# Two attentions on one core: K and V of three batch-head pairs read with an outermost source dimension of 4, 4 and 2

## The chip, the cores and the metric

The kernel runs on one core of a Trainium2 chip. The metric is the device time of one execution in microseconds (us). A core has engines that run side by side: TensorE (PE, its weight loads shown as PEld), VectorE (DVE), ScalarE (ACT), GpSimd (POOL) and SyncE (SP). SP computes nothing; here it issues nearly all transfers. The transfers themselves run on 16 DMA engines, which are something else than the five above: "DMA engine" always means one of the 16 below.

## The reference, cut to what matters

Two attention blocks with a cached K and V, put side by side:

```python
def block(x, k_cache, v_cache, wq, wo):          # x: [16, 32, 1024], Dh = 128, 32 query heads
    q = (x @ wq) split into heads                # [16, 32, 32, 128]
    k, v = each cached head repeated for its query heads   # block A: 4 cached heads, block B: 32
    scores = q @ k^T * 128 ** -0.5               # over Sk = 1024 keys
    o = softmax(scores) @ v
    return (heads of o joined) @ wo              # [16, 32, 1024]
out = concatenate([block(A), block(B)], axis=-1)
```

Only the caches matter here. Block A reads 16 batches x 4 heads of K and V, each [1024 keys, 128] in bf16, 256 KB. Block B reads 16 x 32 of them, 256 MB in all. Softmax and the sum over keys do not depend on the order of the keys, as long as K and V of one batch and head are in the same order.

## The kernel before, in words

The work is cut into 128 steps. Step t has one "quad" of block A (a batch b, a cached head s, and four of the eight query heads that share it, so two quads in a row share one K and V) and, every second step, a pair of quads of block B with four K tiles and four V tiles of 512 KB.

**Loads.** A 512 KB tile of block B goes to 128 partitions with 4096 contiguous bytes each (`st_dmaKB` L904, `st_dmaVB` L949). K and V of block A go to 128 partitions with 2048 contiguous bytes each (`st_dmaKA` L885, `st_dmaVA` L892): partition p takes keys 8p to 8p+7. There are 64 loads of either kind. Weights are loaded in pieces of 256 and 512 KB (L708, L789, L799). Block B's K tiles have 8 buffers, its V tiles 6, block A's K and V two each, `KA_sb` and `VA_sb`, used in turn.

**What is done with them.** A K tile of block A is transposed by PE (L963) and evacuated to `KTA_sb`; scores are made by PE (L989), the row maximum by DVE (L1029), the exponential by ACT (L1042), P is transposed (L1054), and multiplied with V (L1074). A K tile of block B is transposed in place by DVE (L970), then scores (L1018), the same maximum and exponential, transposes (L1088) and the product with V (L1108). Projections stand at L729, L748 and L817.

**The order.** The program records every operation with what it reads and writes. `list_schedule` then places them one by one by modelled durations (a table for the engines; for transfers `dma_time`, bytes in packets over 16 DMA engines) and priorities, and this fixes the order of instructions on each engine. Waits follow from the order: a load waits on a semaphore of PE, ACT or DVE for its buffer to be free, and its first user waits for the load's own semaphore, which counts to 16. All these loads are issued by SP in one queue, in a fixed order, so that a load whose buffer is not free holds up those behind it. POOL issues seven of the output stores (L841).

Quads of block A are numbered by head first: quad t has s = t // 32 and b = 4 * ((t // 8) % 4) + (t % 8) // 2.

Of the kernel before, what the change touches and what calls it, by code (L numbers as in the profile page):

```python
# [546 lines left out]
def build(nc, pa, pb, out):  # L547
# [9 lines left out]
    NCH = Sk // P  # L557
# [22 lines left out]
    pr = Prog()  # L580
    stack = contextlib.ExitStack()
    with stack:
        def sb(name, shape, dt):
            return stack.enter_context(nc.sbuf_tensor(name, shape, dt))
# [20 lines left out]
        KA_sb = sb("KA_sb", [P, 2, NCH, Dh], BF)  # L605
        VA_sb = sb("VA_sb", [P, 2, NCH, Dh], BF)
# [257 lines left out]
        def mk_quadB(t):  # L864
# [13 lines left out]
            q.kid = ("B", t)  # L878
            return q

        def st_dmaKA(q):
            if not q.kv_new:
                return
            sl = q.kvslot
            pr.add("sp", lambda e: e.dma_start(KA_sb[:, sl, :, :], pa["k"][q.b, q.s].rearrange("(p c) d -> p c d", c=NCH)),  # L885
                   writes=[("KA", sl)], dma_key=f"ka{sl}", name="ka_dma", dur=Sk * Dh * 2, wtag={("KA", sl): q.kid})

        def st_dmaVA(q):
            if not q.kv_new:
                return  # L890
            sl = q.kvslot
            pr.add("sp", lambda e: e.dma_start(VA_sb[:, sl, :, :], pa["v"][q.b, q.s].rearrange("(p c) d -> p c d", c=NCH)),  # L892
                   writes=[("VA", sl)], dma_key=f"va{sl}", name="va_dma", dur=Sk * Dh * 2, wtag={("VA", sl): q.kid})

        def tile_src(key, x):
# [336 lines left out]
        def quadA_all(q):  # L1232
            t = q.t
            if q.kv_new:
                n1 = nextA(t, 1)
                if n1 is not None:
                    st_ktrA(n1)
                    n3 = nextA(t, 3)
                    if n3 is not None:
                        st_dmaKA(n3)  # L1240
                if n1 is not None and t >= 1:
                    st_dmaVA(n1)
            st_scoresA(q)
            st_max(q)
            st_exp(q)
            st_ptr(q)
            st_pev(q)
            st_pvA(q)
            st_recip(q)
            st_norm(q)  # L1250
            st_otr(q)
# [9 lines left out]
        for x in range(4):  # L1261
            st_dmaKB(x)
        st_dmaKA(quadsA[newA[0]])
        st_dmaVA(quadsA[newA[0]])
        for x in range(4):
            st_dmaVB(x)
        wo_loadB(0)
        lazy_pop(100)
        if len(newA) > 1:
            st_dmaKA(quadsA[newA[1]])  # L1270
            st_dmaVA(quadsA[newA[1]])
# [81 lines left out]
        if SCHED:  # L1353
            pr = pr.list_schedule()
# [10 lines left out]
def bass_concat_heads__gqa_block_cached__mha_block_cached__near_ridge_kernel(nc, A_x, A_k_cache, A_v_cache, A_wq, A_wo, B_x, B_k_cache, B_v_cache, B_wq, B_wo, out):  # L1365
    build(nc, dict(x=A_x, k=A_k_cache, v=A_v_cache, wq=A_wq, wo=A_wo),
          dict(x=B_x, k=B_k_cache, v=B_v_cache, wq=B_wq, wo=B_wo), out)
# [28 lines left out]
```

## Time and profile before

| what | value |
|---|---|
| time, median of 3 runs | 850.13 us (849.5 to 851.82) |
| time of the profiled execution | 851.77 us |
| its span, first to last instruction | 850.0 us (1.77 us lie around it) |
| busy share of the span: PE, DVE, ACT | 92%, 86%, 73% |
| granted TensorE clock | 0.998 |
| read from HBM, written | 337.64 MB, 2.10 MB |
| mean rate of all DMA | 402 GB/s |
| DMA queue of SP's loads, share of 16 DMA engines | 99.8% |

How to read it. Busy times are sums over an engine's instructions. The DMA share is the time that packets took, over 16 DMA engines and the span; a packet here is one contiguous run, 4096 or 2048 bytes for the loads above, and the next packet of an engine can start a few nanoseconds before the last one's end, which is why shares can pass 100%. "Landing" is the time at which a load's semaphore reaches its full count. Beside its views the trace holds a record of each DMA packet (queue, start, duration, size, but not which of the 16 engines) and the times of the sixteen increments of each load's semaphore, one from each DMA engine; they are called the packet records and the landing records below.

### The profile page before, as it was taken

The numbers are of one execution on the slowest core, as the hardware profiler recorded it, in microseconds if no ns is written. First come the engines' busy times: TensorE is split into PE (matmuls) and PEld (weight loads), VectorE is DVE, ScalarE is ACT, GpSimd is POOL, SyncE is SP. The second block draws the span as 40 slices with busy tenths as digits, with TensorE's granted clock in tenths as the row PEclk, the third lists the DMA queues.
The fourth block names the chain that finished last, engine by engine and source line by source line (L and its number), as shares of the span: only waits on it lengthen the run. The fifth ranks groups of instructions, "written<-read, shape, count | busy, mean of one in ns | idle before, by whom it ended". The sixth has DMA issues, their size and how long they took to land.

```text
span 850.0 us, 29762 instructions
## 1 busy us (share of the span) xinstructions
PE 781.1 (92%) x13056; PEld 519.9 (61%) x13056; DVE 734.1 (86%) x1025; ACT 622.9 (73%) x1356; POOL 6.1 (1%) x20
## 2 busy tenths in 40 slices
PE   6988989999899999999998998999999998989886
PEld 3456666666666566676565665566656666666654
DVE  1499898897898899998999789998899889998995
ACT  3378887876778767877777777686777758787864
POOL 1000000000000000000000000000000000000000
PEclk9999999999999999999999999999999999999999
DMA  9999999999999999999999999999999999999994
GB/s 331 415 404 411 412 411 416 415 400 354 409 414 411 415 412 411 415 397 413 408 416 414 413 406 403 415 403 414 413 404 411 410 411 407 416 415 414 416 417 187
DMA packets 112208, 341.68 MB, mean 402 GB/s; under 512 B 12048, under 2 KB 12304, under 8 KB 112080
## 3 DMA queue, kind: packets, MB, share of 16 engines
q1 hardware_dynamic: 111520, 337.95, 99.8%
q8 instruction: 103, 1.69, 0.7%
q0 software_dynamic: 560, 1.84, 0.5%
q14 instruction: 25, 0.20, 0.1%
HBM read 337.64 MB, written 2.10 MB: 400 GB/s over the span
## 4 chain that ended last, share of the span: by engine, by line
PE 53%; DVE 17%; DMA 15%; ACT 12%; issue 2%; SPq 1%; DVEq 0%; ACTq 0%
PE psum L1108 10%; PE psum L817 9%; DVE stat L1029 8%; ACT P_sb L1042 7%; DVE KB_sb L970 6%; DMA KB_sb<-in_B_k_cache_dram 6%; DMA VB_sb<-in_B_v_cache_dram 5%; PE psum L1018 5%; PE psum L1054 5%; PE psum L748 4%; PE psum L1088 4%; PE psum L989 4%; PE psum L729 4%; PE psum L1074 3%; PE psum L963 2%; DMA wq_sb<-in_B_k_cache_dram 2%
## 5 line engine op out<-in xcount | busy, mean ns | idle before, releaser
L1029 DVE TENSOR_REDUCE stat<-psum 128x1 f32<-128x1024 f32 x256 | 302.9, 1209 | 42.2 <-PE psum L989 25.3
L1042 ACT ACTIVATE P_sb<-psum,stat 128x1024 bf16<-128x1024 f32 x246 | 275.2, 1119 | 70.7 <-DVE stat L1029 67.8
L970 DVE STREAM_TRANSPOSE KB_sb<-KB_sb 128x1024 f32<-128x1024 f32 x240 | 289.7, 1226 | 17.3 <-DMA KB_sb<-in_B_k_cache_dram 16.8
L645 ACT COPY PT_sb<-psum 128x512 f32<-128x512 f32 x223 | 129.5, 598 | 39.7 <-PE psum L1088 22.2
L1108 PE MATMUL psum<-VB_sb,PT_sb 64*64 64x256 bf16 x3584 | 116.9, 271 | 11.9 <-ACT P_sb L1042 6.9
L1108 PEld LDWEIGHTS psum<-VB_sb,PT_sb 64*64 64x64 bf16 x3584 | 96.6, 107 | 33.0 <-issue 29.5
L1167 ACT ACTIVATE O_sb<-psum,stat 128x128 bf16<-128x128 f32 (+1 forms) x203 | 80.8, 418 | 35.4 <-PE psum L1074 16.1
L1054 PE MATMUL psum<-id,P_sb 128*128 128x128 f32 x512 | 88.5, 296 | 4.3 <-ACT P_sb L1042 3.0
L989 PE MATMUL psum<-KTA_sb,QT_sb 128*128 128x512 bf16 x256 | 82.0, 383 | 5.8 <-ACT P_sb L1042 2.6
L1054 PEld LDWEIGHTS psum<-id,P_sb 128*128 128x128 f32 x512 | 73.7, 208 | 19.5 <-ACT P_sb L1042 7.9
L1074 PE MATMUL psum<-VA_sb,PT_sb 128*128 128x128 bf16 x1024 | 77.8, 219 | 4.6 <-ACT P_sb L1042 1.9
L1088 PE MATMUL psum<-id,P_sb 128*128 128x128 f32 x472 | 78.1, 288 | 4.1 <-ACT P_sb L1042 1.1
L1074 PEld LDWEIGHTS psum<-VA_sb,PT_sb 128*128 128x128 bf16 x1024 | 62.5, 98 | 28.3 <-issue 12.3
L1018 PE MATMUL psum<-KB_sb,QR 32*32 32x512 bf16 x3840 | 72.7, 395 | 6.2 <-ACT P_sb L1042 5.4
L1088 PEld LDWEIGHTS psum<-id,P_sb 128*128 128x128 f32 x472 | 64.8, 193 | 20.1 <-ACT PT_sb L645 4.5
L748 PE MATMUL psum<-wq_sb,xT_sb 128*128 128x512 bf16 x256 | 73.0, 392 | 3.3 <-DMA wq_sb<-in_B_wq_dram 2.8
L817 PE MATMUL psum<-woB_sb,OTB_sb 128*128 128x512 bf16 x256 | 66.3, 380 | 3.6 <-ACT P_sb L1042 1.6
L817 PE MATMUL psum<-woA_sb,OTA_sb 128*128 128x512 bf16 x256 | 62.8, 380 | 2.2 <-ACT P_sb L1042 1.9
L1018 PEld LDWEIGHTS psum<-KB_sb,QR 32*32 32x32 bf16 x3840 | 43.6, 89 | 32.5 <-ACT P_sb L1042 9.8
L729 PE MATMUL psum<-xT_sb,wq_sb 128*128 128x512 bf16 x192 | 53.3, 379 | 0.5 <-ACT P_sb L1042 0.3
L1042 ACT ACTIVATION_READ_ACCUMULATOR P_sb<-psum,stat 128x1 f32 x246 | 49.6, 202 | 0.0
L829 DVE TENSOR_TENSOR acc<-acc,psum 128x512 f32<-128x512 f32 x64 | 41.2, 674 | 4.2 <-PE psum L817 4.2
(74 smaller groups left out, 718.3 us busy)
## 6 DMA issues: line engine op xcount, KB each, us to landing
KB_sb<-in_B_k_cache_dram SPq DMA_DIRECT2D x240, 512.0 KB, 9.6
VB_sb<-in_B_v_cache_dram SPq DMA_DIRECT2D x234, 512.0 KB, 9.2
KA_sb<-in_A_k_cache_dram SPq DMA_DIRECT2D x64, 256.0 KB, 8.4
VA_sb<-in_A_v_cache_dram SPq DMA_DIRECT2D x64, 256.0 KB, 8.7
wq_sb<-in_B_wq_dram SPq DMA_DIRECT2D x16, 512.0 KB, 8.1
woB_sb<-in_B_wo_dram SPq DMA_DIRECT2D x32, 256.0 KB, 9.8
woA_sb<-in_A_wo_dram SPq DMA_DIRECT2D x32, 256.0 KB, 10.0
wq_sb<-in_B_k_cache_dram SPq DMA_DIRECT2D x16, 512.0 KB, 11.4
```

The lines of the kernel that those rows point to most:

```text
L645: return e.copy(dst, src) if hasattr(e, "activation") else e.tensor_copy(dst, src)
L748: last = e.matmul(bank(v)[:, 0:CW], xT_sb[:, 1, j, G * P:(G + 1) * P], wq_sb[:, j, mh * CW:(mh + 1) * CW], start=(j == 0), stop=(j == DJ - 1))
L817: last = e.matmul(bank(v)[:, 0:OUTW], OT[:, gp, hh, :], wo_[:, hh, oh * OUTW:(oh + 1) * OUTW], start=(hh == 0), stop=(hh == nh - 1))
L970: pr.add("dve", lambda e: e.transpose(tile_k(x).bitcast(F32), tile_k(x).bitcast(F32)), writes=[home_k(x)], name="KBt_tr", rtag={home_k(x): ...
L989: pr.add("pe", lambda e, u=u: e.matmul(bank(vS[u]), qt[:, q.b, q.hh0:q.hh0 + 4, :].rearrange("p a q -> p (a q)"), KTA_sb[:, sl, u * 512:(u ...
L1018: last = e.matmul(bank(q.vS[g2])[32 * x:32 * x + 32, :].rearrange("p (s j) -> p s j", s=16), lhsT, rhs, start=(fp == 0), stop=(fp == 3), t ...
L1029: pr.add("dve", lambda e: e.tensor_reduce(stat[:, vst.idx, 0:1], both(vS), AXIS.XY, ALU.max, negate=True), writes=vS + [vst], name="max")
L1042: return e.activation(dst, src, ACTF.Exp, bias=stat[:, vst.idx, 0:1], scale=1.0, accum_out=stat[:, vst.idx, 1:2])
L1054: last = e.transpose(bank(vb)[:, m * P:(m + 1) * P], p32[:, m:Sk // 2:NPK], id32[:])
L1074: last = e.matmul(bank(vb)[:, 0:Dh], ptc_of(vPT, c, 0, P), VA_sb[:, kvs, c, :], start=(c == 0), stop=(c == NCH - 1))
L1088: last = e.transpose(bank(vb)[:, m * P:(m + 1) * P], p32[:, 4 * h + m:Sk:8], id32[:])
L1108: last = e.matmul(bank(q.vbo)[n0:n0 + 64, 0:2 * Dh].rearrange("p (i d) -> p i d", i=2), pt[e0:e0 + 64, c // 2, n0:n0 + 64, c % 2], v2[e0:e ...
```

## The change

For (s, b) = (0, 3), (2, 3) and (1, 5), K and V of block A are read through another source pattern. With x = 4, "(v x c) d -> x v (c d)" makes the source [4][32][1024 elements] with steps of 1024, 4096 and 1: partition 32x + v now takes the keys from 8(4v + x) on. With x = 2 it is [2][64][1024]. The destination is still 128 partitions of 2048 contiguous bytes, the source runs are still 2048 bytes, and K and V of a pair get the same order. All other loads keep source and destination with 128 outermost.

```diff
+        FEW = {(0, 3): 4, (2, 3): 4, (1, 5): 2}
+
+        def a_src(key, q):
+            src = pa[key][q.b, q.s]
+            if (q.s, q.b) in FEW:
+                return src.rearrange("(v x c) d -> x v (c d)", x=FEW[(q.s, q.b)], c=NCH)
+            return src.rearrange("(p c) d -> p (c d)", c=NCH)
+
         def st_dmaKA(q):
...
-            pr.add("sp", lambda e: e.dma_start(KA_sb[:, sl, :, :], pa["k"][q.b, q.s].rearrange("(p c) d -> p c d", c=NCH)),
+            pr.add("sp", lambda e: e.dma_start(KA_sb[:, sl, :, :].rearrange("p c d -> p (c d)"), a_src("k", q)),
...
-            pr.add("sp", lambda e: e.dma_start(VA_sb[:, sl, :, :], pa["v"][q.b, q.s].rearrange("(p c) d -> p c d", c=NCH)),
+            pr.add("sp", lambda e: e.dma_start(VA_sb[:, sl, :, :].rearrange("p c d -> p (c d)"), a_src("v", q)),
```

The scheduler sees the same bytes and the same dependencies, so the order of instructions and the waits on every engine are the same in both programs; line numbers after L880 stand eight higher in the changed one. The six loads are, in the trace of before, those that SP issues at 40.28 us (K of (0, 3)), 65.81 (its V), 268.73 (K of (1, 5)), 289.95 (its V), 444.21 (K of (2, 3)) and 467.35 (its V).

## The prediction

> **What bounds the kernel now.** I read the page's DMA part first, because the change touches only loads, then the groups, the waits and the chain, and then single stretches.
>
> ```profile
> PE 781.1 (92%) x13056; PEld 519.9 (61%) x13056; DVE 734.1 (86%) x1025; ACT 622.9 (73%) x1356; POOL 6.1 (1%) x20
> ...
> q1 hardware_dynamic: 111520, 337.95, 99.8%
> q8 instruction: 103, 1.69, 0.7%
> ...
> PE 53%; DVE 17%; DMA 15%; ACT 12%; issue 2%; SPq 1%; DVEq 0%; ACTq 0%
> ```
>
> SP's loads fill the 16 DMA engines, while PE and DVE are nearly as full: two limits lie close together. The q8 row is instruction fetches: 0.7% of 16 x 850 us is 95 us in 103 packets, 0.92 us each, and they run on the same DMA engines.
>
> ```profile
> L970 DVE STREAM_TRANSPOSE KB_sb<-KB_sb 128x1024 f32<-128x1024 f32 x240 | 289.7, 1226 | 17.3 <-DMA KB_sb<-in_B_k_cache_dram 16.8
> ```
>
> This is where a late load is felt: the transposes of block B's K stood 16.8 us for their tiles. The next lines are from the tile view of KA_sb.
>
> ```profile
> L885 SPq DMA_DIRECT2D KA_sb<-in_A_k_cache_dram x64: 327/328/1682, 4.2 to 782.4; - x64
> ...
> DMA to landing us min/median/max: 5.8/8.4/14.4
> ```
>
> A load of 256 KB takes 8.4 us from issue to landing, though its own packets take 0.64 us of each DMA engine (below): it stands in a queue. The queue is never empty for long between 20 and 830 us.
>
> **The DMA engines are uneven.** In the packet records a 2048-byte packet takes 84 ns and the next starts 80 ns after it; 4096 bytes take 159 and 156. A load gives each DMA engine 8 packets: 0.64 us for 256 KB, 1.25 for 512 KB. The landing records tell how far apart the 16 finish one load: 1.8 us at 20 us, 3.1 at 50, 4.3 at 300, 4.9 at 500 and at 830. The distance grows in jumps of one DMA engine by about 1.4 us, each at a fetch, and the fetches' durations repeat with period eight: eight DMA engines take turns, 13 fetches and some 18 us each. The other eight run ahead, find the queue empty more often (33 us between 20 and 830 us, against some 13 on the last one: 31 us beyond its packets' own time, less 18 of fetches), and a load has landed only when the last of the late ones has.
>
> **What the change does, step by step.** It adds no instruction and no wait, and SP's order is the same. Loads with 128 rows outermost are dealt in equal shares over 16 DMA engines. Four or two outermost rows cannot be dealt over sixteen; no load of before has fewer than 128, so the trace does not show the case. From below: dealt as before, 0. From above: confined to four and two DMA engines. I take confinement, since all loads are dealt by whole outermost rows.
>
> The Trainium skill (DMA: Bandwidth & Descriptors, "Why a DMA increments its semaphore by 16 and not by 1") says that the largest number up to 16 that divides the outermost sizes of both sides gives the DMA engines used, and that they are the lowest-numbered. By that it is 4 and 2; no run here shows it yet.
>
> Confined to four, a load costs 32 x 80 ns = 2.56 us on them, 1.92 more than now; confined to two, 64 x 80 = 5.12, 4.48 more. The DMA engines left out save 0.64 each time, 3.84 over six loads. Over the run two DMA engines get 4 x 1.92 + 2 x 4.48 = 16.6 us more, two get 4 x 1.92 - 2 x 0.64 = 6.4 more.
>
> The six tiles themselves have room. From landing to first use the records give 9.8, 12.7, 21.9, 10.3, 14.3 and 1.2 us in the order of issue. What counts is what stands behind them in the same queues.
>
> Which DMA engines are meant, the trace does not number. At the first load eight start by 1.83 us and eight some 0.3 us later. The five that the first hold-ups (three before 5 us) and fetches hit can be followed back to the second eight by their delay from last packet to increment. If the first eight are the low numbers, the small loads fall on DMA engines that run ahead. I take that.
>
> Then I carry two numbers from load to load: what the favoured ones have gained in backlog (less the time for which they stood empty before), and the 0.64s that the late ones save.
>
> - (0, 3): backlog 1.92 after K at 40 us; 0.78 of it is worked off in the gap at 54 us, so 3.06 after V at 66 us. The late ones were 2.2 behind there: landings come 0.8 later for some 10 us, then about 1 us earlier.
> - (1, 5): the early ones stand empty for only 0.5 us between 272 and 300 us. Backlog 8.4 against a distance of 3.7: every landing behind V is **4.7 us late**.
> - (2, 3): when it comes, 5.5 of that is left; with two more loads 9.4 against 3.6, so 5.8 late on the two, for a tile with 1.2 us of room.
> - After that the backlog is worked off: 3.3 late at 560 us, 0.6 at 670, and 2.8 **early** at 790, where only the late ones' relief is left.
>
> ```profile
> 268.73 0.33 SPq L885 DMA_DIRECT2D KA_sb<-in_A_k_cache_dram  x1
> ...
> 289.95 0.33 SPq L892 DMA_DIRECT2D VA_sb<-in_A_v_cache_dram  x1
> ```
>
> Between these two issues SP issues 21 other loads, all in the queues behind the first.
>
> How much of 4.7 us reaches the end? Half of block B's K tiles are used within 0.12 us of landing.
>
> ```profile
> 297.76 0.69 DVE L829 TENSOR_TENSOR acc<-acc,psum 128x512 f32<-128x512 f32 x1 [0.23 <-PE psum L817]
> 298.37 0.34 DVE L1158 RECIPROCAL stat<-stat 128x1 f32<-128x1 f32 x4
> 298.73 2.49 DVE L970 STREAM_TRANSPOSE KB_sb<-KB_sb 128x1024 f32<-128x1024 f32 x2
> ```
>
> The two tiles of the last row landed at 298.71 and 299.95, and each is transposed 0.02 us later; no cover lies there. A delay is won back only where compute now waits for loads. Behind 300 us those waits come to about 5 us in all (landing less the end of the instruction before, summed over the tiles that are used at once), and only some stand where landings are already early again. So 4.7 less 1 to 3 stays, with (0, 3)'s gain of about 1 before it: an estimate of 2 to 3.5, and I take **3 us**, the row nearest being the late landings between 290 and 340 us, which meet compute without room. On the profiled execution, 851.77 us (a span of 850.0 and 1.77 around it), that is 854.8; on the median shown, 1.64 below, **853 us**.
>
> One cost is left beside it: SP's issue takes up to 2.9 us where some 11 loads are outstanding (0.43 otherwise), and a backlog of 64 packets on two DMA engines can bring that about at 271 to 276 us. All of SP's issues stand behind it. The cover is the other DMA engines' queue of 3 to 8 us, so I put it at 0; at the most it is one such hold-up per load, 2 x 2.9 us, and it is in the upper part of the range.
>
> The Trainium skill (Runtime: NRT & Kernel Launch, "Instruction fetch mechanics") calls the cost of a fetch mostly hidden. On PE that may be so; for the DMA engines the landing records disagree, with 1.4 us a fetch. Were it 0, there would be no distance to fill, and (1, 5) would cost 8.4 us in place of 4.7.
>
> **Rivals.**
> 1. *Relief wins* (the other side). Landings behind 690 us are 2.8 us early in the sum above. If compute can run faster than the trace lets it, the delay of the middle is caught up by then and the end comes 2.8 us early: **847.3**. For it: DVE is empty 9% of 300 to 700 us, so a few microseconds are there. Against it: PE is busy 93 to 97% there, and waits on DMA are few. It decides for this side if the delay still in compute at 690 us is below about 1 us; it also holds if the favoured DMA engines were further ahead than 3.7 us.
> 2. *The loads fall on late DMA engines.* Then nothing absorbs them: two late ones get 16.6 more, less what they stand empty for: 10 to 16, **863**. Against it: the order of the first starts.
> 3. *It does not do what it says*: dealt over 16 all the same, **850.1**. For it: packets keep size and number.
>
> **Chances.** Forecast 0.49 (its own range 850.5 to 857, with SP's hold-up as upper part), relief 0.28, no effect 0.10, late DMA engines 0.13. A measurement of this kernel tells about 0.3%, 2.55 us, from no change. Faster by more: 0.26 from relief. Within: 0.10 + 0.13 of the forecast + 0.02 of relief = 0.25. Slower: 0.36 of the forecast + 0.13 = 0.49. The range reaches from relief's lower end, 846.5, to 859; left out are most of the second rival and little else.
>
> **What would show it.** Packets stay at 111520 on q1. The landing records of the six loads show four and two increments that come late, the others at once; if all sixteen climb as before, rival 3 holds. Loads behind 290 us take 4 to 5 us longer to landing than now, up to about 340 us, and DVE's waits for KB_sb grow there; if they do not, the favoured DMA engines had more room. K or V of these pairs should hold up nobody but at 478 us. From 700 us on, landings nearer to issue than now tell of the relief. The prediction is wrong if the small loads spare the queue they stand in, or if compute wins back the middle.

## The result, and the profile after

The changed kernel takes **873.96 us** (median of 4, 871.93 to 875.68) against 850.98 (median of 4, 849.5 to 853.23): 1.0265 times as long, 95% interval 1.0244 to 1.0286, some 23 us slower. The forecast was 853.0 and the range ended at 859. The profiled execution took 875.68, its span is 873.8.

Two lines of the page of before, for comparison. Each digit, and each number, is one of 40 equal slices of the span:

```profile
PEclk9999999999999999999999999999999999999999
GB/s 331 415 404 411 412 411 416 415 400 354 409 414 411 415 412 411 415 397 413 408 416 414 413 406 403 415 403 414 413 404 411 410 411 407 416 415 414 416 417 187
```

From the page of the changed kernel, the lines that answer to those of before:

```profile
PE 790.4 (90%) x13056; PEld 526.4 (60%) x13056; DVE 733.1 (84%) x1025; ACT 622.5 (71%) x1356; POOL 6.1 (1%) x20
...
PEclk9998999999999889999999999999999999999999
DMA  9999999999999999999999999999999999999994
GB/s 336 414 384 340 353 398 416 414 415 366 414 416 395 351 343 346 405 406 407 408 415 387 383 401 396 404 406 414 413 413 413 408 414 404 414 416 414 404 417 179
...
q1 hardware_dynamic: 111444, 337.95, 98.7%
q8 instruction: 103, 1.69, 0.7%
...
PE 56%; DVE 15%; DMA 13%; ACT 12%; issue 2%; SPq 1%; DVEq 0%; ACTq 0%
```

Three things are to be seen. **One**: q1 has 76 packets fewer than before (111520). That is 4 x 12 + 2 x 14: each four-row load lost 12 of its 16 semaphore packets of 4 bytes, each two-row load 14. The loads were confined to four and two DMA engines, as predicted. **Two**: the DMA row stays at 9 everywhere, yet the GB/s row falls in the slices (21.8 us each) at 44 to 109 us (384, 340, 353), at 284 to 349 (351, 343, 346) and at 459 to 502 (387, 383), that is, from each pair on. Busy DMA engines that move less: packets must have become longer, as the packet records below show. **Three**: PE's busy time grew by 9.3 us with the same instructions, and PEclk shows an 8 in three slices, where every digit of before is 9.

The waits of block B's K transposes, on the page's line of the group (before: 16.8 us):

```profile
L978 DVE STREAM_TRANSPOSE KB_sb<-KB_sb 128x1024 f32<-128x1024 f32 x240 | 288.6, 1225 | 27.9 <-DMA KB_sb<-in_B_k_cache_dram 27.6
```

Two lines of the tile view of KA_sb. Its median from issue to landing, 7.6 us, looks like relief beside the 8.4 of before and is not: a semaphore that once counted a confined load has fewer updates than 16 a load, and the view leaves out all loads of its buffer. The line speaks of the 32 loads into the other buffer, none of the six among them; before, the same 32 had a median of 8.1 us.

```profile
L893 SPq DMA_DIRECT2D KA_sb<-in_A_k_cache_dram x64: 327/328/1312, 4.7 to 806.5; - x64
...
DMA to landing us min/median/max: 5.3/7.6/14.1
```

**Packets.** While the packets of one of the six loads are being moved, most packets of the queue are slow, those of other loads too. At K of (2, 3), from 466.5 to 471.2 us, the medians are 129 ns for 2048 bytes (84 before) and 236 for 4096 (159), 95% of either size are slow (over 95 and 170 ns), and the rate is 282 GB/s; at K of (1, 5), from 281.3 to 288.0 us, 113 and 204 ns, 81% and 74%. The slow stretch ends within about half a microsecond of the landing each time. Summed over the run, 2048- and 4096-byte packets took 196 us more than 84 and 159 ns before, and 416 us after: per DMA engine, 12.3 and 26.0 us. Of what was added, 220 us, 154 lie in the six slow stretches, 9.6 us per DMA engine. Most of the rest lies in stretches such as 84 to 112 us, where the medians are 84 and 159 ns again, single packets take up to 1 us, and the DMA share falls below 1 (0.53 at 84 to 86): there the queue has run thin.

**Landings**, load by load against before: each of the six sets back all that follow, by 2.7 and 3.4 us at (0, 3), 5.9 and 6.0 at (1, 5), 1.3 and 1.9 at (2, 3), 21.2 us in all. Behind V of (1, 5) the distance is 17.1 us, up to K of (2, 3) it stays between 16.6 and 18.9, and at the last store it is 23.8.

**PE.** In stretches of two microseconds. The columns are the stretch, then busy time (and instructions) of PE, PEld, DVE, ACT and POOL, the granted clock, the DMA share, GB/s. First behind V of (0, 3), then behind V of (1, 5):

```profile
76.00:78.00 2.00, 1.07 (x10) 0.70 (x7) 1.74 (x2) 2.00 (x6) 0.00 (x0) 1.00 1.03 345
78.00:80.00 2.00, 0.00 (x0) 0.00 (x0) 0.86 (x1) 1.50 (x3) 0.00 (x0) 0.88 1.02 416
80.00:82.00 2.00, 0.20 (x5) 0.23 (x9) 0.61 (x5) 0.00 (x0) 0.00 (x0) 0.50 1.03 422
82.00:84.00 2.00, 2.00 (x44) 2.00 (x40) 0.00 (x0) 0.00 (x0) 0.00 (x0) 0.50 1.03 422
84.00:86.00 2.00, 2.00 (x31) 1.34 (x24) 0.00 (x0) 0.31 (x2) 0.00 (x0) 0.50 0.53 215
```

```profile
320.00:322.00 2.00, 0.00 (x0) 0.00 (x0) 2.00 (x3) 0.45 (x1) 0.00 (x0) 0.97 1.05 411
322.00:324.00 2.00, 1.19 (x48) 0.82 (x64) 1.99 (x5) 1.89 (x4) 0.00 (x0) 0.50 1.04 407
324.00:326.00 2.00, 2.00 (x48) 1.18 (x30) 1.23 (x3) 0.25 (x1) 0.00 (x0) 0.50 1.06 412
326.00:328.00 2.00, 2.00 (x48) 1.68 (x44) 2.00 (x3) 1.32 (x3) 0.00 (x0) 0.50 0.51 200
328.00:330.00 2.00, 2.00 (x37) 1.71 (x30) 1.25 (x3) 0.75 (x2) 0.00 (x0) 0.83 0.13 51
```

The order is the same both times: PE stands still, the granted clock falls to 0.50 for 6.8 us, buffers come free late, and then the DMA engines run dry (shares 0.53 and 0.13). The timeline names the late loads: at 77.5 us a V tile of block B that PE itself needs, at 317.6 us a K tile that DVE is to transpose (PE, behind DVE and ACT, stands 5.2 us). A third standstill, 3.5 us from 285.2 us on behind K of (1, 5), waits for a piece of the weights (woB_sb).

```profile
81.81 3.63 PE L1116 MATMUL psum<-VB_sb,PT_sb 64*64 64x256 bf16 x64 [4.30 <-DMA VB_sb<-in_B_v_cache_dram]
...
296.22 1.94 PE L1116 MATMUL psum<-VB_sb,PT_sb 64*64 64x256 bf16 x64
```

```profile
319.16 1.25 DVE L978 STREAM_TRANSPOSE KB_sb<-KB_sb 128x1024 f32<-128x1024 f32 x1 [4.90 <-DMA KB_sb<-in_B_k_cache_dram]
```

The same form of 64 matmuls takes 3.63 us behind the standstill at 77.5 us and 1.94 at full clock.

So the 23.8 us of span divide by PE: 9.3 us more busy time (the same matmuls, some at half clock) and 14.5 us more standstill (span less busy time: 68.9 before, 83.4 after). By the clock row in stretches of one microsecond, clock lost sums to 15.4 us, against 1.8 before.

### The profile page after: what moved, and what is told of

Same layout as the page of the kernel before. It is cut to its first block, busy times and chain, and to the rows that moved or that the text cites. A ratio compares the mean times of both kernels' runs of the same rounds, so it can differ in the third digit from the quotient of the medians.

```text
span 873.8 us, 29762 instructions
## 1 busy us (share of the span) xinstructions
PE 790.4 (90%) x13056; PEld 526.4 (60%) x13056; DVE 733.1 (84%) x1025; ACT 622.5 (71%) x1356; POOL 6.1 (1%) x20
## 4 chain that ended last, share of the span: by engine, by line
PE 56%; DVE 15%; DMA 13%; ACT 12%; issue 2%; SPq 1%; DVEq 0%; ACTq 0%
PE psum L1116 10%; PE psum L817 9%; DVE stat L1037 7%; DMA KB_sb<-in_B_k_cache_dram 7%; ACT P_sb L1050 7%; PE psum L1026 6%; DVE KB_sb L978 5%; PE psum L1062 5%; PE psum L729 5%; PE psum L1096 5%; PE psum L997 4%; PE psum L748 4%; PE psum L1082 4%; DMA VB_sb<-in_B_v_cache_dram 2%; PE psum L971 2%
## 5 line engine op out<-in xcount | busy, mean ns | idle before, releaser
L1116 PE MATMUL psum<-VB_sb,PT_sb 64*64 64x256 bf16 x3584 | 120.3, 276 | 14.6 <-ACT P_sb L1050 6.4
L1116 PEld LDWEIGHTS psum<-VB_sb,PT_sb 64*64 64x64 bf16 x3584 | 99.1, 109 | 36.2 <-issue 32.3
L1062 PE MATMUL psum<-id,P_sb 128*128 128x128 f32 x512 | 89.6, 299 | 6.4 <-ACT P_sb L1050 5.1
L1026 PE MATMUL psum<-KB_sb,QR 32*32 32x512 bf16 x3840 | 73.2, 398 | 10.1 <-ACT P_sb L1050 9.3
L1096 PE MATMUL psum<-id,P_sb 128*128 128x128 f32 x472 | 78.9, 290 | 3.7 <-ACT P_sb L1050 1.1
L1082 PEld LDWEIGHTS psum<-VA_sb,PT_sb 128*128 128x128 bf16 x1024 | 63.5, 99 | 30.9 <-issue 12.3
L817 PE MATMUL psum<-woB_sb,OTB_sb 128*128 128x512 bf16 x256 | 68.1, 387 | 7.0 <-DMA woB_sb<-in_B_wo_dram 3.8
## 6 DMA issues: line engine op xcount, KB each, us to landing
woA_sb<-in_A_wo_dram SPq DMA_DIRECT2D x32, 256.0 KB, 10.3
```

The costliest lines, as they stand in the source:

```text
L817: last = e.matmul(bank(v)[:, 0:OUTW], OT[:, gp, hh, :], wo_[:, hh, oh * OUTW:(oh + 1) * OUTW], start=(hh == 0), stop=(hh == nh - 1))
L1026: last = e.matmul(bank(q.vS[g2])[32 * x:32 * x + 32, :].rearrange("p (s j) -> p s j", s=16), lhsT, rhs, start=(fp == 0), stop=(fp == 3), t ...
L1062: last = e.transpose(bank(vb)[:, m * P:(m + 1) * P], p32[:, m:Sk // 2:NPK], id32[:])
L1082: last = e.matmul(bank(vb)[:, 0:Dh], ptc_of(vPT, c, 0, P), VA_sb[:, kvs, c, :], start=(c == 0), stop=(c == NCH - 1))
L1096: last = e.transpose(bank(vb)[:, m * P:(m + 1) * P], p32[:, 4 * h + m:Sk:8], id32[:])
L1116: last = e.matmul(bank(q.vbo)[n0:n0 + 64, 0:2 * Dh].rearrange("p (i d) -> p i d", i=2), pt[e0:e0 + 64, c // 2, n0:n0 + 64, c % 2], v2[e0:e ...
```

## The experiments

Times below are compared with runs of the kernel before on the same chip; a plus sign is the difference that the ratio gives. Medians of packets are those of the slow stretch at the load named. Three theories: **C**, confinement itself slows all packets; **W**, the steps in the source do; and, formed after the first four runs, **P**: two DMA engines writing the same partitions at a time do. **Q** stands for the plain queue of a few DMA engines, without slow packets; the first two expectations call it B.

**1. Confined, but neighbouring rows** (e1_gap). The patterns become [4][32] and [2][64] with steps of one row inside and 40 or 72 rows outside.

```diff
-        FEW = {(0, 3): 4, (2, 3): 4, (1, 5): 2}
+        FEW = {(0, 3): (4, 40, 1), (2, 3): (4, 40, 1), (1, 5): (2, 72, 1)}
...
+            x, pitch, step = FEW[(q.s, q.b)]
...
+            grid = rows[r0:r0 + x * pitch].rearrange("(x w) f -> x w f", w=pitch)
+            return grid[:, 0:step * (P // x):step]
```

> Same three pairs, still four, four and two outermost rows, but each DMA engine now walks 32 or 64 neighbouring rows (64 or 128 KB without a step) in place of rows 8 or 4 KB apart; the blocks lie 40 and 72 rows apart so that they stay separate dimensions, hence these three pairs attend to other keys than the reference's. Theory C (company): in the trace of the changed kernel all packets on all DMA engines run slower while a confined load is under way (84 ns grows to some 135, 159 to some 270; 410 GB/s falls to some 255 with four, 310 with two DMA engines in it), and it is the confinement itself that does it; then nothing changes here: 871 to 877 us, slow packets as before. Theory W (walk): the step of 8 or 4 KB in the source does it; then packets stay at 84 and 159 ns and only the longer queue of two to four DMA engines is left: 853 to 866 us. Theory B (queue only, the slow packets being a side show): 871 to 877 us with packets at 84 and 159 ns.

874.35 us (868.85 to 875.93; ratio 1.0254, 1.0209 to 1.0299), packets as slow as in the change (K of (2, 3): 129 and 252 ns, 129 and 236 there). The walk in the source is not what makes the confined loads slow: W falls for them, and B, which had expected 84 and 159 ns, falls as well.

**2. Steps, but 16 DMA engines** (e2_step16): the same lines with (16, 36, 4) twice and (16, 20, 2).

> The steps without the confinement: 16 outermost rows, so all 16 DMA engines take a share, but each walks its 8 packets in steps of 8 KB (two pairs) or 4 KB (one pair); these three pairs attend to other keys than the reference's. Theory C: packets at 84 and 159 ns, 850 to 852 us, no difference from the kernel before. Theory W: packets run slow while these six loads are under way, 84 to some 135 ns; at the loss per byte of the changed kernel (about 2 us of all DMA engines per load) 858 to 863 us, at the least 853. Theory B: as C.

857.87 us (854.55 to 860.12; ratio 1.0080, 1.0054 to 1.0107), and packets slow at each load: 120 and 232 ns at V of (1, 5). C and B had expected nothing. Either the walk costs after all, or something that 16 outermost rows share with four.

**3. Only (1, 5)** (e3_one2): `FEW = {(1, 5): 2}`.

> Only the pair (1, 5), two outermost rows, is left of the change. In the trace of the changed kernel landings fall back by 5.9 us at its K and by 5.5 to 6 at its V. Theories C and W: those stay, nothing is worked off: 851 plus 11 to 12, 860 to 864 us. Theory of the prediction (most of the extra work is taken up by DMA engines that run ahead): 853 to 855 us.

860.97 us (859.58 to 864.16; ratio 1.0120, 1.0091 to 1.0150): +10.3, as C and W expected, and not the +3 of the prediction. The profiled execution is 7.8 us longer than that of before, and from 310 us on its landings stay 6.8 to 7.9 us behind, to the end: nothing is won back.

**4. Ten patterns in one run** (e4_probes): ten entries in `FEW`.

> Ten pairs spread over the run, each with another source pattern for K and V; only the packet times during each load count, not the end. In order of time: 16 rows 2 KB apart with inner steps of 32 KB; 8 rows (steps of 16 KB); 4 blocks of 32 neighbouring rows; 2 blocks of 64; 4 rows with steps of 8 KB (as in the change); 16 rows with inner steps of 8 KB; 16 with inner steps of 4 KB; 2 rows with steps of 4 KB (as in the change); 8 blocks of 16 neighbouring rows; 32 rows. The blocks and the 16 rows with 8 and 4 KB steps read other keys than the reference's. Theory C: slow packets at 8, 4 and 2 outermost rows whether in blocks or in steps, least at 8 and most at 4; none at 16 and 32. Theory W: slow packets wherever there are steps of 8 or 4 KB, at 16 outermost rows too; none in blocks of neighbouring rows. Semaphore packets: 4 bytes each, as many as DMA engines take part, by either theory 8, 4 and 2 in place of 16.

The time, 891 us, does not matter. Slow: 16 rows with steps of 2 KB between DMA engines (some 120 and 200 to 230 ns at K and V), 8, 4 and 2 rows, blocks and steps alike, and 16 rows with steps of 8 and 4 KB. Not slow: **32 rows** (no such stretch at all). C and W both fall: 16 rows leave no DMA engine out, and blocks have no steps. What 16, 8, 4 and 2 have in common, and 32 and 128 have not, is the destination: with 32, the unit dealt out is four partitions; with 16, eight.

**5. Loads alone** (e5_lab). SP's program for each test is company, probe, company; `pieces` makes the probes onto some partitions alone:

```python
def pieces(r, first, x, v, n):
    m = x * v
    return [(T[first:first + m, f, :], keys[r + m * f:r + m * (f + 1)].rearrange("(v x) f -> x v f", x=x)) for f in range(n)]
...
for c in range(COMPANY * company):
    e.dma_start(C[:, c, :], big[t]).then_inc(sems[i], 16)
...
for dst, source in probe(128 * i):
    e.dma_start(dst, source).then_inc(sems[i], 16)
```

> Loads alone, nothing of the reference is computed: 18 tests one after the other, each with 6 loads of 512 KB (4096-byte packets, the company), a probe of 256 KB in 2048-byte packets, 6 more loads of 512 KB, and a wait for all; the last four have no company. Probes in order: whole tile with 128, 32, 16, 8, 4, 2 outermost rows; pieces of 32 partitions from 8 outermost rows at partitions 0, 64 and 4; pieces of 16 from 4 rows at 0, 16 and 32; pieces of 8 from 2 rows at 0 and 8; without company 128 rows, 4 rows, pieces of 16 at 0 and 16. So far: 16 rows are slow as well, whatever the walk in the source, 32 are not. Theory P (destination): each group of four partitions is normally written by one DMA engine; a load is slow, and slows all, where DMA engines write groups that belong to others. Then no slow packets with 128 and 32 rows and with pieces at 0 and 32; slow ones with 16, 8, 4, 2 rows and pieces at 64, 4, 16 and 8. The Trainium skill (DMA: Bandwidth & Descriptors, The descriptor swizzle) has the map used here: partitions 0 to 3 and 32 to 35 go by the first DMA engine, 4 to 7 and 36 to 39 by the second, and so on, 64 to 127 by the other eight. Theory C (confinement): pieces of 8, 4 and 2 rows are slow wherever they are written. Without company P gives 4 rows and pieces at 16 between 84 ns and the slow time, C 84 ns.

Median packets of the probe, and of the company while the probe runs:

| probe | probe, ns | company, ns |
|---|---|---|
| 128 rows; 32 rows | 84; 84 | 159; 159 |
| 16; 8; 4; 2 rows | 84 (a tenth over 158); 154; 147; 122 | 185; 282; 274; 226 |
| 8 rows onto 32 partitions at 0; at 64 | 84; **160** | 159; **297** |
| 4 rows onto 16 partitions at 0; at 32; at 16 | 84; 84; **167** | 159; 159; **312** |
| 8 rows onto 32 partitions at 4 | 84 (a tenth over 152) | 159 |
| no company: 128 rows; 4 rows; at 0; at 16 | 84 in all | - |

The same pattern is at full speed onto partitions 0 to 15 and at half speed onto 16 to 31. P holds and C falls. Two lines of P missed. Without company it had allowed for slow packets with 4 rows and with the pieces at 16, and the medians there are 84 ns, as with C: a conflict seems to need a second writer that is at work, which the last run tests. And the pieces at 4 were nearly undisturbed. By P's own reading, each of eight DMA engines writes its neighbour's four partitions there while the neighbour writes the next, so that few groups have two writers at a time. The two-row pieces tell nothing: their sixteen issues left the queue empty (some 95 GB/s). The Trainium skill (DMA: Bandwidth & Descriptors, "The descriptor swizzle") gives each DMA engine of a 128-partition load two groups of four partitions, 32 apart; 0, 32, 64, 16 and the 32 rows came out as that map says. No record here shows directly which DMA engine wrote what.

**6. The change with 32 rows** (e6_rows32): `FEW = {(0, 3): 32, (2, 3): 32, (1, 5): 32}`.

> The change with 32 outermost rows for all three pairs in place of 4 and 2: keys reordered in the same manner, steps of 64 KB in the source, all 16 DMA engines. Theory P: each DMA engine keeps its groups of four partitions, packets at 84 and 159 ns, 850 to 852 us, no difference from before. Theory W (source steps): some of the loss of the run with 16 rows and steps of 8 and 4 KB (7 us) stays, 853 to 858.

851.17 us (848.64 to 853.43, 12 runs; ratio 1.0005, 0.9991 to 1.0019). The keys are reordered as in the change, and nothing is lost. Its page:

```profile
GB/s 339 415 413 415 415 412 416 415 395 377 415 415 411 416 412 414 416 400 406 413 415 413 414 404 401 416 406 413 414 406 413 413 404 406 416 416 414 416 416 194
...
q1 hardware_dynamic: 111520, 337.95, 99.9%
```

No dip stands at 44 to 109, at 284 to 349 or at 459 to 502 us, and all semaphore packets are back.

**7. The queue alone** (e7_copy). Ahead of each of the six loads, which are as before:

```diff
+                rows = pa[key][q.b + 1, q.s].rearrange("(p c) d -> p (c d)", c=NCH)[0:x * n]
+                e.dma_start(copy[r0:r0 + x * n].rearrange("(v x) f -> x v f", x=x), rows.rearrange("(v x) f -> x v f", x=x))
```

> The kernel before, all its loads dealt over 16 DMA engines as ever, with six copies from DRAM to DRAM ahead of the six loads: 24 packets of 2 KB on each of four DMA engines (4 copies) and 56 on each of two (2 copies), so 1.92 and 4.48 us of extra queue on the lowest DMA engines, as the prediction counted, without a write to SBUF. Theory P1: the queue is mostly taken up as the prediction carried it, and the rest of the 23 us is the slowing of all packets: 853 to 856 us. Theory Q: nothing of a backlog is ever worked off without holding the kernel: 16.6 us less the 3 to 4 us by which the favoured DMA engines run ahead, 861 to 865. Both hold only if the packets of the copies and of the loads beside them stay near 84 and 159 ns.

862.64 us (861.3 to 866.33; ratio 1.0128, 1.0107 to 1.0149): +10.9, theory Q. The medians of the copies' and the company's packets are 84 and 159 ns at all six loads. This is the prediction's own case without the slow packets, but for one thing: copies do not take the 0.64 us a load (3.84 us in all) off the other DMA engines that a confined load takes off them. It cost three to four times what the prediction gave it. SP's timeline at V of (1, 5), and the stretches behind it:

```profile
295.99 0.61 SPq L896 DMA_DIRECT2D copy<-in_A_v_cache_dram  x1
296.64 4.26 SPq L897 DMA_DIRECT2D VA_sb<-in_A_v_cache_dram  x1
```

```profile
300.00:308.00 8.00, 7.57 (x113) 5.76 (x113) 7.40 (x13) 6.02 (x13) 0.00 (x0) 1.00 0.95 338
308.00:312.00 4.00, 2.88 (x14) 1.25 (x14) 0.00 (x0) 0.97 (x2) 0.00 (x0) 1.00 1.02 400
312.00:318.00 6.00, 1.63 (x64) 0.90 (x64) 4.91 (x7) 2.33 (x4) 0.00 (x0) 0.86 1.03 401
```

One issue lasted 4.26 us (0.43 in the median), all of SP's issues stood behind it, the other DMA engines lost their queue (338 GB/s), and PE stood 5.4 us from 310.9 us on. Landings fell back by 6.2 us over the two loads of (1, 5), from 4.6 to 10.8, and stayed 10.8 behind at 380 us. The profiled execution is the slowest of the six, 14.6 us above that of before, so its distances add up to more than the 10.9.

**8 and 9. 16 and 8 rows** (e8_rows16, e9_rows8): `FEW` with 16, and with 8, three times.

> The change with 16 outermost rows for all three pairs: no DMA engine has more to do than before, but each writes eight neighbouring partitions, half or more of which belong to others. Theory P: the slow packets cost all DMA engines 0.7 to 0.9 us a load (excess of all packets in the probe run, 11.4 and 14.7 us over 16 DMA engines), 855 to 857 us. If only confinement costs: 850 to 852.

> The change with 8 outermost rows for all three pairs. Theory P: in the tests of loads alone 8 rows ended 1.8 us later than 32; six times that, 859 to 863 us. By queue alone (0.64 us extra on eight DMA engines, six times, less the distance): 850 to 853.

858.39 us (856.57 to 859.69; ratio 1.0079, 1.0056 to 1.0102) and 863.42 (860.99 to 864.47; ratio 1.0135, 1.0111 to 1.0160). With 16 rows every DMA engine has its usual share, and only the slow packets are left: +6.6 us, a little above what P expected. By all packets' excess it is 19.3 - 12.3 = 7.0 us per DMA engine, so here the slowing reaches the end one for one. With 8 rows it is +11.7, just above P's range and far from the 850 to 853 of the queue alone.

**10. Loads alone, one DMA a probe** (e10_lab2).

```python
def one(first, x, row):
    rows = A_v_cache.rearrange("b s k d -> (b s k d)")[0:4 * x * row].rearrange("(v x f) -> x v f", x=x, v=4)
    return [(T[first:first + 4 * x, 0:row], rows)]
```

> Loads alone again, nothing of the reference is computed: 8 probes, the list run twice, each between 8 and 8 loads of 512 KB and followed by a wait; each probe is one DMA now, so that issue takes nothing from it. In order: a normal tile (128 rows, 256 KB); 4 outermost rows onto partitions 0 to 15, 64 KB per DMA engine in packets of 16 KB; the same onto 16 to 31; the same onto 64 to 79; the tile with 4 rows of the change; 2 rows onto partitions 0 to 7, 128 KB per DMA engine in packets of 32 KB; the same onto 8 to 15; the same onto 64 to 71. Theory P: at partition 0 the company stays at 159 ns and the test ends later than the normal one by the queue alone, 1.9 us for four and 4.5 us for two; at 16 and 64, 8 and 64 the company slows (some 312 ns with four, 226 with two) and the test ends later by 3.5 to 4.5 and 6 to 7 us. Theory C: the same at every partition.

Packets of 16 KB took 612 ns at 0 and 1224 and 1217 at 16 and 64; of 32 KB, 1213 at 0 and 2474 and 2477 at 8 and 64; the company 159, and 320 to 333. The second round of the list agrees within 1.4% on the probes' packets. In the stretches (last columns clock, DMA share, GB/s) four DMA engines at 0, 16 and 64 and two at 0, 8 and 64:

```profile
37.50:39.50 2.00, 0.00 (x0) 1.00 1.04 428
64.00:67.00 3.00, 0.00 (x0) 1.00 0.98 199
92.00:95.00 3.00, 0.00 (x0) 1.00 1.04 212
147.00:151.00 4.00, 0.00 (x0) 1.00 1.03 421
176.00:182.00 6.00, 0.00 (x0) 1.00 1.04 204
208.00:214.00 6.00, 0.00 (x0) 1.00 1.03 202
```

Busy to the full in all six, with half the bytes in four. Against the normal test the ends are 1.9 us later at 0, 5.0 and 3.5 to 3.9 at 16 and 64 (four), and 3.0, 7.9 and 8.0 to 8.5 (two); the tile of the change with 4 rows 3.5. P holds; the queue alone of two is less than the 4.5 expected, the conflict more than 6 to 7.

**11. Control for the copies** (e11_copy16): the same copies, x = 16.

> Control for the run with copies: the same six copies from DRAM to DRAM with nearly the same bytes (96 packets of 2 KB each for the two pairs, 112 for the one), dealt over all 16 DMA engines, 6 or 7 packets each, 0.48 to 0.56 us. If the 10.9 us of the confined copies are the queue of the few DMA engines (theory Q), these cost only their share of all sixteen, 6 x 0.5 = 3 us at most: 851 to 855 us. If they are the copies themselves (their writes to DRAM, their issue), 860 to 864.

853.98 us (851.56 to 856.31; ratio 1.0027, 1.0011 to 1.0044), +2.3: what the copies cost as such, bytes and issue, is a small part of the 10.9.

**12. Only the four-row pairs** (e12_fours): `FEW = {(0, 3): 4, (2, 3): 4}`.

> Only the pairs (0, 3) and (2, 3), four outermost rows, are left of the change. The pair (1, 5) alone cost 10.3 us of the 23. If delays add up because none is won back (theory Q with the slow packets), 12 to 13 us are left for these four loads, 863 to 865 us. If an early delay is won back later, less: the pair (0, 3) would be gone by 270 us, and (2, 3) alone gives 855 to 858.

860.74 us (859.14 to 862.32; ratio 1.0106, 1.0082 to 1.0131), +9.0, between the two expectations. With the +10.3 of (1, 5) alone it makes 19.3 of 23; the intervals of the three allow for plain addition.

**13. Does it take a busy owner?** (e13_owners). Company by eight DMA engines, `C[0:32, c, :]` from eight outermost rows, or by 16.

> Loads alone, nothing of the reference is computed: the probe of two outermost rows (128 KB on each of two DMA engines, packets of 32 KB) onto partitions 0 to 7, 8 to 15 and 64 to 71, first in the company of loads by the first eight DMA engines alone (32 partitions, 8 outermost rows, 4096-byte packets, each DMA engine on its own four partitions), then of loads by all 16; the list twice. With all 16 in company the last run had 159 ns at 0 and 320 to 333 at 8 and 64. Theory P (a conflict with a busy owner): with eight in company nothing is slow at 0 and at 64, whose owners have nothing to do, and at 8 the probe doubles. If only the DMA engines that meet at the same partitions are slowed, two of the six others in company are slow at 8, a quarter or less of the company's packets; if a conflict holds up all, nearly all of them are. If instead writing foreign partitions is slow by itself, 64 is as slow as 8.

Probe of two DMA engines at partitions 0, 8 and 64, first in the company of eight, then of sixteen (columns as in run 10):

```profile
13.00:17.00 4.00, 0.00 (x0) 1.00 0.48 172
38.00:44.00 6.00, 0.00 (x0) 1.00 0.51 123
65.00:69.00 4.00, 0.00 (x0) 1.00 0.43 169
96.00:100.00 4.00, 0.00 (x0) 1.00 1.01 408
136.00:142.00 6.00, 0.00 (x0) 1.00 1.01 201
178.00:184.00 6.00, 0.00 (x0) 1.00 1.00 201
```

The third line decides: at 64, with eight in company, the probe's packets keep 1.22 us and 10% of the company's or fewer are slow (over 170 ns; of that company without a probe, about 15% are); with sixteen, when the owners of 64 to 71 work, the probe's packets take 2.44 us and all of the company's in the stretch are slow. It takes a busy owner. And more are held up than the two that meet: with eight, 60 to 69% of the company's packets are slow at 8 while the probe is at work, where a quarter had to be if only two were; with sixteen, all in the stretch. That 60 to 69% is less than the "nearly all" of the other branch; why is open.

## Why the prediction was wrong, point by point

- **What bounds the kernel**: right. Two limits lie close, and a late load finds no cover.
- **Confinement to four and two DMA engines**: right, and the rule of the Trainium skill that the prediction cites with it. The landing records show one update 1.0 us after issue and four or two late ones. "Packets stay at 111520" was wrong by the 76 semaphore packets.
- **"32 x 80 ns = 2.56 us", "64 x 80 = 5.12"**: the step that failed first. The 80 ns came from loads whose DMA engines keep to partitions of their own. In the six slow stretches the 2048-byte packets, the confined ones and some of other loads, took 102 to 129 ns (medians), and, what no term of the sum held, the 4096-byte packets of the other loads went from 159 to between 187 and 240 meanwhile. With 16 rows, where the slowing comes without a longer queue, it costs 6.6 us. The packet time of a confined load was the unknown; the prediction bounded only who does the work (0 or confined) and not how fast it runs.
- **The six tiles have room**: right. Of their own users only that of V of (2, 3) was waited for, 2.1 us by PE at 501.5 us, and this is the one that the prediction had named (478 us in the trace of before).
- **The loads fall on DMA engines that run ahead**: half right. With (1, 5) alone, K's two increments came 10.1 and 10.8 us after issue; 64 packets of 112 ns are 7.2, so both began 2.9 and 3.6 after it, where the load before it landed between 3.0 and 6.7: among the first. At K of (0, 3), one of four landed at 11.0 and three at 8.6 to 9.0. The distance took up some 3 us once, not again. It is no fixed stock either: the prediction quotes 3.1 us at 50 and 4.3 at 300, and the same landing records of before give 2.3 at 200 and 3.0 at 400.
- **"every landing behind V is 4.7 us late"**: for the queue alone not far off, 6.2 in the run with copies. **"4.7 less 1 to 3 stays", 3 us reach the end**: the second step that failed. All 6.2 stayed, and (0, 3), behind which landings were to come 1 us early, left them 5.7 late some 30 us after its V, and 4.6 at 270 us. The queue alone cost 10.9 instead of 3. A backlog was worked off, but by the other DMA engines running dry: tiles land late, PE stands still, its clock halves, buffers come free late, SP waits. The waits that compute already had, 5 us behind 300 us, were no reserve: with PE 90% busy nothing was won back up to the end.
- **SP's hold-up put at 0, at most 2.9 a load**: it came in the run with copies, 4.26 us in one issue. In the change it is hardly to be seen: 2.8 us at 314.7 us, where the same load took 2.3 before, and the longest issue is 2.98 us in either kernel.
- **Relief from 700 us on**: landings did come nearer to issue, but because issue had become later. Load by load behind 727 us, issue was mostly some 24 us later than before and landing 20 to 22.6 (the last stores apart). Nearness to issue alone does not tell relief.
- **Rivals**: none held. "Late DMA engines", 863, has the size of the queue alone by another mechanism; no effect at all is what 32 rows give, not 4.

How the 23 us add up: queue alone 10.9 (up to 2.3 of it the copies as such), slow packets alone, with 16 rows, 6.6. The rest, 5.5 us or some more, is not shown by a run of its own. Two estimates from the rows point at where it lies. The slow stretches of the change added 9.6 us per DMA engine, those of 16 rows 7.1. And the slowing makes the short queues longer: some 32 x 46 ns four times and 64 x 30 ns twice, 10 us on the two DMA engines that take part in all six. The two overlap, so they are not to be added. What half clock adds in each is read from the clock row, not tested by taking it away.

## What to carry to other kernels

Before a load is given another outermost size, ask which partitions each DMA engine will write, not only how many take part: a pattern that keeps four-partition units dealt as in a full 128-row load (32 rows here) cost nothing here, and one that puts a second writer beside a busy one slowed all transfers while it lasted (421 to 428 GB/s down to about 200 in the loads alone, 268 to 318 in the changed kernel). A bound for the unknown must cover the speed of the new packets and of their company, and the nearest undisturbed row is only its lower end. Where the DMA queue and PE are both above 90%, as here, count a delay in full and look for PE standstills of some microseconds, behind which the clock row falls.

## What the runs showed of the hardware that was not expected

- Two DMA engines writing the same partitions at a time: their packets take twice as long (16 KB: 612 to 1224 ns), and so do those of the others (159 to 320 to 333); without a busy owner the probe's packets keep their time (1.22 us). That it is the partitions which are shared is inferred from where the slow probes wrote; no record shows a DMA engine's partitions. Why the others are held up too stays open; nothing in the records shows the path.
- Granted clock 0.50 in stretches of some 3.4 or 6.8 us (1.7 or 3.4 us of clock lost): six in the changed kernel, one before, none with 32 rows (the last 0.3 us of a span left out). The three long ones begin in PE standstills of 4.3, 3.5 and 5.2 us; two short ones come in or behind standstills of 2.6 and 2.1 us, and the third, at 728 us, behind nothing longer than 0.81, so no threshold is read from here. The Trainium skill (TensorE: Matmul & The Clock Gate, "Part 1: The HAM clock gate") gives half rate and a window of 3.4 us; the trace agrees with both.
